# FNet mixing and an ELU feed-forward layer: the second batch's sequence transform in quarter form, and weight sums of two chunks at a time

## The chip, the cores and the metric

The kernel runs on one core of a Trainium2 chip. A core has a matrix engine (TensorE, PE), a vector engine (VectorE, DVE), a scalar engine (ScalarE, ACT), a general engine (GpSimd, POOL) and a queue for transfers (SyncE, SP). Each engine works through its own list of instructions, and semaphores order the lists against each other. The metric is device time in microseconds (us), the median of several executions; lower is better.

## The reference

`x` has 8 batches of 3008 rows (the sequence) by 256 channels in float32; `w_in` (256 x 2048) and `w_out` (2048 x 256) arrive in float64.

```python
X = np.fft.fft(x, axis=1)            # along the sequence, 3008 points
X = np.fft.fft(X, axis=2)            # along the channels, 256 points
y = X.real.astype(np.float32).reshape(8 * 3008, 256)
h = y @ w_in
g = np.where(h > 0.0, h, np.exp(np.minimum(h, 0.0)) - 1.0)
out = (g @ w_out).astype(np.float32)
```

## The kernel before

**The sequence transform.** The channel transform is multiplied into `w_in` once, when the weights are prepared (`fold_chunk`, into `Wc` and `Ws`). What is left is a real transform along the sequence for each batch, in two parts (cosines with channels folded evenly, sines with channels folded oddly) and each of these for even and odd frequencies: four transforms a batch, which the code names by `ri` (0 cosine, 1 sine) and `kodd` (0 even, 1 odd frequencies). GpSimd and VectorE first add and subtract rows of `x` that share a cosine, so that fewer rows are left to be multiplied. TensorE then multiplies the folded rows, which are its stationary operand, with a table of cosines, and VectorE unfolds the products into two ring buffers, `Rr` and `Ir`, of which each column is one frequency. A transform is done in two halves; a half is a group of matmuls into one bank `H`.

**Half form.** Batches 0 and 1 use it. The rows are split into six classes by their place modulo 8 and 4, folded twice, and lie in tiles `eo` of 128 rows; a half is three matmuls with the table `MC`: of 188, 188 and 376 columns in a first half, of some 376 columns each in a second half. In batch 1 the folding is 30 GpSimd operations (`mirror_folds`), spread over slots 6 to 30.

**Quarter form.** Batches 2 to 7 use it. The rows are split into eight classes (by their place modulo 8), of 96 and 94 rows; `near` (`far` = 0) and `far` tiles hold four classes each, as `xq0` to `xq3`. `load_quarter` and `load_odd` load them, by SyncE or by GpSimd's indirect transfers. GpSimd adds mirrored rows (`mirror_sum`), VectorE adds or subtracts the halves (`half_sum`, L627), GpSimd folds the channels (`channel_fold`, L630), ScalarE copies one column that has no partner (`channel_edge`, L633), VectorE and GpSimd combine classes (`quarter_pairs`, `shift_pairs`, `turn_pairs`; L911 is the vector engine's turn), and a half is then four matmuls of at most 95 columns with the smaller table `QM`.

**Slots.** The feed-forward layer works on 47 tiles of 256 frequencies, in 376 slots: a slot is one tile with two of the 16 blocks of 128 hidden features. In a slot TensorE forms `H` from `Rr` with `Wc` (called P here) and from `Ir` with `Ws` (Q); VectorE or ScalarE takes the part E between the two (`even_part`, L1401 on VectorE); VectorE forms the mirrored frequency's row as 2E - H (`h_minus`, L1415); ScalarE computes the exponentials (`below_plus` is the first of them, `G<-H`; then `M<-G`, `G<-G`, `M<-M`); VectorE finishes the ELU (`g_plus`, `g_minus`, L1431). TensorE then multiplies `G` with `w_out` into `pA` to `pD` (X below) one to two slots later. Slots 0 to 15 alternate between tiles 0 and 1, since the weights are still arriving, and multiply with plain products. From slot 16 a slot uses seven products (Winograd's form): GpSimd makes four sums of blocks of `G` in each slot (`G<-G`), and needs sums of `w_out`'s blocks (`sum_weights`, into `WT`), which it forms once, at slots 13 to 17: four operations for each of eight pairs of blocks.

**The weights.** They are turned from float64 to float32 on the chip in chunks, beside slots 0 to 14. Of each chunk VectorE takes two steps (`pow<-raw` L408 and `w<-raw` L420), ScalarE three (`pow<-pow,ebias`, `raw<-raw`, `w<-w`), GpSimd one (`w<-raw,w`), VectorE one (`pow<-raw,pow`, L462), GpSimd one (`w<-w,pow`). The four chunks 4 to 7 of `w_in` are also folded with the channel transform (`raw<-w` on GpSimd, a fold on TensorE, `Wsc<-H` on ScalarE). `spread_last_row` then sends one row of the result through memory into the columns `wex` (SyncE, `wx<-Wsc` at L673 and `wex<-wx` at L676), which E (and from slot 16 a seed on ScalarE) needs.

**Order.** The program is a list of events with a time each, in units of `T` = 4.8 us a slot; they are sorted by time and issued in that order. The times place instructions against each other on an engine's list; they do not make anything wait. So each engine's list is fixed by the table of times, and what an engine does when follows from the lists and the semaphores. The first 33 us have a table of their own (`FRONT`), in which `L` and `L0` to `L3` are the transfers of batch 1's rows.

## Time and profile before

| | |
|---|---|
| median of 3 runs | 1906.94 us (1906.89 to 1907.48) |
| profiled execution, its own time | 1907.16 us |
| its span in the trace | 1905.4 us |
| TensorE, matmuls | 1898.3 us busy, 8972 matmuls |
| VectorE | 1232.0 us busy |
| ScalarE | 1391.4 us busy |
| GpSimd | 1353.1 us busy |

The span is the time between the first and the last instruction in the trace; 1.76 us of the profiled execution's own time lie outside it. Rows of the trace give the start of a run of like instructions and its length in us, the engine, the source line, what is written and read, and how many instructions the run has (`x4`); in square brackets stands how long the engine was idle before and what it waited for. Each matmul stands in the trace as two records, so that `x6` is three matmuls. Since matmuls overlap, the price of a group of matmuls is the distance from its start to the next group's start, not its length. Before slot 34 and in the last slots TensorE is idle for some 10 us altogether; between them it never stops for more than a fraction of a microsecond.

### The profile page before, as it was taken

Reading aid. Unit: us, or ns where it says so; the run is one execution under the profiler, and the core shown is the slowest. Engines: PE = TensorE matmul, PEld = TensorE weight load, DVE = VectorE, ACT = ScalarE, POOL = GpSimd, SP = SyncE. Lnnn points to the kernel's source line nnn. Section 1 sums busy time; section 2 is a strip of 40 time slices with the busy share of each in tenths; the row PEclk is TensorE's granted clock in tenths of the full one; section 3 lists DMA queues with packets and bytes.
Section 4 is the critical chain, followed back from the end, with each engine's and each line's share of the span. In section 5 each row is a group of like instructions: output and inputs, shape, how many; then the busy total and the mean of one; then the engine's idle time right before and its main releaser. Section 6 shows DMA issues by size and latency. Waiting matters only on the chain.

```text
span 1905.4 us, 28620 instructions
## 1 busy us (share of the span) xinstructions
PE 1898.3 (100%) x8972; PEld 1656.8 (87%) x8972; DVE 1232.0 (65%) x2174; ACT 1391.4 (73%) x2803; POOL 1353.1 (71%) x1846
## 2 busy tenths in 40 slices
PE   9999999999999999999999999999999999999999
PEld 6888888888888888888888888888888888888887
DVE  8755555667666676667766677666776667655445
ACT  5767667777777777777777777777777777777775
POOL 4888658786687766777667777687766777556664
PEclk9999999999999999999999999999999999999999
DMA  8145211211011110211102111022110210100101
GB/s 340 45 33 43 55 24 45 53 24 36 12 44 41 32 33 12 47 40 30 31 19 50 35 27 31 13 56 44 24 24 16 55 21 15 17 12 15 20 11 24
DMA packets 278901, 73.66 MB, mean 39 GB/s; under 512 B 254382, under 2 KB 268972, under 8 KB 278750
## 3 DMA queue, kind: packets, MB, share of 16 engines
q1 hardware_dynamic: 270110, 61.40, 15.9%
q0 software_dynamic: 6464, 10.18, 1.7%
q8 instruction: 71, 1.16, 0.3%
q14 instruction: 80, 0.66, 0.1%
q10 hardware_dynamic: 2176, 0.26, 0.1%
HBM read 46.92 MB, written 24.80 MB: 38 GB/s over the span
## 4 chain that ended last, share of the span: by engine, by line
PE 96%; DVE 2%; ACT 1%; issue 0%; DMA 0%; POOL 0%; ACTq 0%; POOLq 0%; DVEq 0%
PE H L621 37%; PE pB L621 17%; PE pD L621 17%; PE pC L621 17%; PE pA L621 9%; DMA xl<-in_x_dram,ix 0%; DVE e L721 0%; ACT G L633 0%; DVE o L721 0%; POOL w L630 0%; DVE G L1431 0%; DVE E L1401 0%; ACT M L633 0%; ACT E L633 0%; DVE pow L462 0%
## 5 line engine op out<-in xcount | busy, mean ns | idle before, releaser
L630 POOL TENSOR_TENSOR G<-G 128x256 f32<-128x256 f32 x1437 | 1047.4, 737 | 498.0 <-DVE G L1431 358.5
L1431 DVE SCALAR_TENSOR_TENSOR G<-G,H 128x512 f32<-128x512 f32 x376 | 258.2, 687 | 554.5 <-ACT G L633 554.5
L633 ACT ACTIVATE G<-H 128x512 f32<-128x512 f32 x376 | 224.5, 597 | 259.0 <-DVE G L1415 255.4
L621 PE MATMUL H<-Rr,Wsc 128*128 128x256 f32 x1504 | 388.7, 381 | 1.0 <-ACT Wsc L633 0.5
L621 PE MATMUL H<-Ir,Wsc 128*128 128x256 f32 x1504 | 386.7, 380 | 0.7 <-DVE E L1401 0.7
L633 ACT ACTIVATE H<-Rb,wex 128x256 f32<-128x256 f32 x720 | 341.2, 474 | 40.0 <-DVE G L1431 21.5
L621 PE MATMUL pC<-G,WT 128*128 128x256 f32 x1440 | 369.8, 379 | 0.0
L633 ACT ACTIVATE E<-H 128x512 f32<-128x512 f32 x360 | 214.5, 596 | 182.0 <-PE H L621 181.7
L621 PEld LDWEIGHTS H<-Ir,Wsc 128*128 128x128 f32 x1504 | 285.6, 190 | 40.6 <-DVE E L1401 1.5
L621 PEld LDWEIGHTS H<-Rr,Wsc 128*128 128x128 f32 x1504 | 281.7, 190 | 43.1 <-issue 2.3
L621 PEld LDWEIGHTS pC<-G,WT 128*128 128x128 f32 x1440 | 274.2, 190 | 36.6
L1415 DVE SCALAR_TENSOR_TENSOR G<-E,H 128x512 f32<-128x512 f32 x376 | 255.0, 678 | 8.4 <-PE H L621 4.3
L1431 DVE SCALAR_TENSOR_TENSOR G<-M,G 128x512 f32<-128x512 f32 x376 | 256.7, 683 | 0.7 <-ACT M L633 0.7
L633 ACT ACTIVATE G<-G 128x512 f32<-128x512 f32 x376 | 235.0, 625 | 0.0
L621 PE MATMUL pA<-G,w 128*128 128x256 f32 x784 | 229.6, 380 | 0.1
L621 PE MATMUL pB<-G,w 128*128 128x256 f32 x784 | 229.5, 379 | 0.0
L621 PE MATMUL pD<-G,w 128*128 128x256 f32 x784 | 229.4, 379 | 0.0
L633 ACT ACTIVATE M<-G 128x512 f32<-128x512 f32 x376 | 224.4, 597 | 2.8 <-DVE G L1415 2.8
L633 ACT ACTIVATE M<-M 128x512 f32<-128x512 f32 x376 | 222.7, 592 | 0.1
L621 PE MATMUL pB<-G,WT 128*128 128x256 f32 x720 | 214.7, 380 | 0.0
L621 PE MATMUL pD<-G,WT 128*128 128x256 f32 x720 | 214.4, 379 | 0.0
L621 PEld LDWEIGHTS pA<-G,w 128*128 128x128 f32 x784 | 149.2, 190 | 20.6 <-DVE G L1431 0.5
(175 smaller groups left out, 1794.3 us busy)
## 6 DMA issues: line engine op xcount, KB each, us to landing
out_dram<-ot SPq DMA_DIRECT2D x496, 32.0 KB
xq<-in_x_dram SPq DMA_DIRECT2D x48, 94.0 KB
out_dram<-ot SPq DMA_DIRECT2D x256, 2.0 KB
Rb<-r SPq DMA_DIRECT2D x10, 376.0 KB
raw<-in_moe_w_in_dram SPq DMA_DIRECT2D x7, 512.0 KB
MC<-dft_mats SPq DMA_DIRECT2D x3, 943.5 KB
xq<-in_x_dram SPq DMA_DIRECT2D x12, 192.0 KB
xq<-in_x_dram SPq DMA_DIRECT2D x36, 64.0 KB
```

The lines of the kernel that those rows point to most:

```text
L621: nc.tensor.matmul(out_, lhsT=lhsT, rhs=rhs, start=start, stop=stop, skip_group_check=True)
L630: pin(nc.gpsimd.tensor_tensor(out=o, in0=a, in1=b, op=op))
L633: pin(nc.scalar.activation(out=o, in_=i, func=func, **kw))
L1415: nc.vector.scalar_tensor_tensor(out=two(S.G[:, 0:512])[:, :, ::-1], in0=two(S.E), scalar=2.0, in1=two(S.H), op0=ALU.mult, op1=ALU.subtract,)
L1431: nc.vector.scalar_tensor_tensor(out=o, in0=e, scalar=-1.0, in1=h, op0=ALU.add, op1=ALU.max)
```

## The change

Batch 1's transform takes the quarter form of batches 2 to 7. `mirror_folds` and its 30 GpSimd operations go; the loads of batch 1's rows, its folds, pairs and halves get places of their own from two tables (`FIRST`, `QUARTERS`), whose numbers are slots. Of the eight half sums two run on GpSimd, six on VectorE. In all batches a half sum is now one operation on two classes (96 x 2 x 256) where it was two (96 x 256 each). `sum_weights` handles two pairs of blocks in one operation: 16 operations of 128 x 256 in place of 32 of 128 x 128, at slots 13.2, 15.1, 16.4 and 17.3. The quarter tables `QM` are loaded at slots 18 to 30 instead of 51 to 60, which batch 2 needs later anyway. The number of halves of batch 1 stays eight; their places go from slots 26, 28, 34, 36, 37, 39, 42, 44 to slots 23, 25, 34, 36, 38, 40, 44, 46.

```diff
-        b11, b12 = w2v[:, 2 * i, 0:128], w2v[:, 2 * i, 128:256]
-        b21, b22 = w2v[:, 2 * i + 1, 0:128], w2v[:, 2 * i + 1, 128:256]
-        W = [t[:, i] for t in WT]
+        w = w2v[:, 2 * i : 2 * i + 4].rearrange("p (n r) (h c) -> p n r h c", r=2, h=2)
+        (b11, b12), (b21, b22) = ([w[:, :, r, h] for h in range(2)] for r in range(2))
+        W = [t[:, i : i + 2] for t in WT]
...
-    def mirror_folds(L):
...
-    def half_sum(kodd, far, h):
+    def half_sum(kodd, far, h, tt=vtt):
...
-        for m in (2 * h, 2 * h + 1):
-            vtt(o[:, 3 - m], a[:, m], b[:, m], ALU.subtract if kodd else ALU.add)
+        m = slice(2 * h, 2 * h + 2)
+        tt(o[:, 2 - 2 * h : 4 - 2 * h][:, ::-1], a[:, m], b[:, m], ALU.subtract if kodd else ALU.add)
...
-    names["L"] = lambda: [open_x(1)] + [state["loads"][n]() for n in (4, 5)]
-    for n in range(4):
-        names[f"L{n}"] = lambda n=n: state["loads"][n]()
+    def load_next(j):
+        load_quarter(1, j, 0)
+        if j in (0, 3):
+            load_odd(1, j, 0)
+
+    names["L"] = lambda: [load_next(0), load_next(3)]
+    names["L0"] = lambda: [quarter_table(), load_next(2)]
+    names["L1"] = lambda: load_next(1)
+    names["L2"] = lambda: [quarter_row(1), load_odd(1, 1, 0)]
+    names["L3"] = lambda: load_odd(1, 2, 0)
...
-    for i in range(8):
-        at((12.9 + 0.5 * i) * T + 3.6, lambda i=i: sum_weights(i))
+    for n, t in enumerate((13.208, 16.4467, 17.2731, 15.0726)):
+        at(t * T, lambda i=2 * n: sum_weights(i))
...
+    FIRST = (((10.3723, 'q', 0), (10.73, 'q', 3), (13.0128, 'q', 1), (11.9409, 'q', 2),
...
+    QUARTERS = ((23, 1, 0, 0, 29), (34, 0, 0, 0, 38), (38, 0, 1, 43, 48), (44, 1, 1, 45, 53))
...
-    at(34 * T, lambda: nc.sync.dma_start(out=twist_tab[0:96], in_=QT_dr.ap()))
-    for n in range(4):
-        at(
-            (51 + 3 * n) * T,
-            lambda n=n: load_quarter_mats(n % 2, n // 2),
-        )
-    first = (6, 6, 7, 7, 7, 7, 7, 8, 8, 8, 9, 9, 9, 9, 12, 15)
...
-    for n in range(30):
-        slot = first[n] if n < len(first) else n + 1
...
-    for step, ri, kodd in ((26, 0, 0), (34, 1, 0), (37, 0, 1), (42, 1, 1)):
-        at_dft(step, 2, 1, ri, kodd, lambda k=2 * ri + kodd: state["EO"][k])
+    at(20 * T, lambda: nc.sync.dma_start(out=twist_tab[0:96], in_=QT_dr.ap()))
+    for ri, kodd, step in ((1, 0, 18), (1, 1, 22), (0, 0, 30.3), (0, 1, 30.4)):
+        at(step * T, lambda ri=ri, kodd=kodd: load_quarter_mats(ri, kodd))
...
+    FAR_LOADS, MIRROR, HALVES, FOLDS, PAIRS = FIRST
+    for dt, fn, *key in FAR_LOADS:
+        at(dt * T, lambda fn={"q": load_quarter, "o": load_odd}[fn], key=key: fn(1, *key, 1))
+    for n, t in enumerate(MIRROR):
+        far, n = divmod(n, 8)
+        at(t * T, lambda n=n, far=far: mirror_sum((0, 3)[n // 4], far, (0, 2, 1, 3)[n % 4]))
+    for t, *key in HALVES:
+        at(t * T, lambda key=key: half_sum(*key[0:3], gtt if key[3] else vtt))
+    for t, ri, *key in FOLDS:
+        at(t * T, lambda ri=ri, key=key: channel_fold(ri, *key))
+        if key[2] and not ri:
+            at(t * T + 0.3, lambda key=key: channel_edge(*key[0:2]))
+    for t, fn, *key in PAIRS:
+        fn = {"p": quarter_pairs, "s": shift_pairs, "t": turn_pairs}[fn]
+        at(t * T, lambda fn=fn, key=key: fn(1, *key))
...
+    for step, ri, kodd, finish, join in QUARTERS:
+        at_quarter(step, 1, ri, kodd, finish, join)
```

Three places of the engines' lists show how the change moves instructions. The first is ScalarE's list around slot 11, whose `below_plus` is `G<-H`; the three rows ahead of it belong to the weights' last chunk of `w_in` (`w1`). Before:

```order
L633 ACTIVATE pow2_785<-pow2_785,ebias_71 128x512
L633 ACTIVATE raw_451<-raw_451 128x512
L633 ACTIVATE w1_450<-w1_450 128x2x256
L633 ACTIVATE G_828<-H_793 128x512
L633 ACTIVATE M_839<-G_828 128x512
```

With the change:

```order
L633 ACTIVATE pow2_807<-pow2_807,ebias_71 128x512
L633 ACTIVATE raw_460<-raw_460 128x512
L633 ACTIVATE w1_459<-w1_459 128x2x256
L633 ACTIVATE e_794<-xq1_529 96x4
L633 ACTIVATE e_847<-xq2_444 96x4
L633 ACTIVATE G_858<-H_815 128x512
L633 ACTIVATE M_877<-G_858 128x512
```

The two edge copies of batch 1's near tiles (`channel_edge`) now stand ahead of slot 11's `below_plus`. Each writes one column of a tile that GpSimd's channel folds write too.

The second is GpSimd's list at the same slots, where `w1` is the same chunk of `w_in` and `w2` a chunk of `w_out`. Before:

```order
L630 TENSOR_TENSOR w2_68<-w2_68,pow2_740 128x512
L630 TENSOR_TENSOR w1_450<-raw_451,w1_450 128x2x256
L630 TENSOR_TENSOR w1_450<-w1_450,pow2_785 128x2x256
L630 TENSOR_TENSOR raw_451<-w1_450 128x256 x2
L630 TENSOR_TENSOR bs_825<-side_768 1x188 x2
```

With the change:

```order
L303 DMA xq3_797<-in_x_dram,ix_66 94x768
L630 TENSOR_TENSOR e_801<-xq2_444 96x256
L630 TENSOR_TENSOR w1_459<-raw_460,w1_459 128x2x256
L630 TENSOR_TENSOR e_794<-xq1_529 96x256
L630 TENSOR_TENSOR w1_459<-w1_459,pow2_807 128x2x256
L630 TENSOR_TENSOR raw_460<-w1_459 128x256 x2
L630 TENSOR_TENSOR e_847<-xq2_444 96x256 x2
L630 TENSOR_TENSOR bs_855<-side_778 1x188 x2
```

Four channel folds of batch 1 now stand among the chunk's steps and right behind them; `e_847`, which ScalarE's second edge copy also writes, stands behind all of the chunk's steps.

The third is SyncE's list at slot 13, with the two transfers of `spread_last_row` for the last chunk. Before:

```order
L673 DMA wx_96<-Wsc_69 1x256
L676 DMA wex_70<-wx_96 128x2x1
L1214 DMA x1_938<-in_x_dram 8x192x1 x4
```

With the change:

```order
L673 DMA wx_96<-Wsc_69 1x256
L319 DMA xq1_929<-in_x_dram 80x2x256
L319 DMA xq1_929<-in_x_dram 14x2x256
L319 DMA xq1_929<-in_x_dram 32x2x256
L676 DMA wex_70<-wx_96 128x2x1
L319 DMA xq1_929<-in_x_dram 15x2x256
```

Three loads of batch 1's far rows now stand between the two transfers.

65 lines of the change are left out of this document (1 added, 64 removed).

## The prediction

> **What bounds the kernel now.** I read the page's busy times first, then its chain of waits, then the trace by stretches of time for each engine.
>
> ```profile
> PE 1898.3 (100%) x8972; PEld 1656.8 (87%) x8972; DVE 1232.0 (65%) x2174; ACT 1391.4 (73%) x2803; POOL 1353.1 (71%) x1846
> ```
>
> ```profile
> PE 96%; DVE 2%; ACT 1%; issue 0%; DMA 0%; POOL 0%; ACTq 0%; POOLq 0%; DVEq 0%
> ```
>
> TensorE is busy for the whole span and carries 96% of the chain that ends last. So two things move the end: matmul time that goes or comes, and any wait that reaches TensorE, since nothing behind such a wait is idle enough to take it up. Relief of the other engines is worth nothing unless one of their results arrives late at TensorE. The sum is made against the profiled execution's own 1907.16 us (span 1905.4 and 1.76 around it); the median is 0.22 lower.
>
> **The matmuls.** The rows of TensorE's timeline, one half of batch 1 of each length and one half of a quarter batch:
>
> ```profile
> 235.49 1.43 PE L621 MATMUL H<-MC,eo 128*128 128x188 f32 x6
> 236.75 1.03 PE L621 MATMUL H<-Rr,Wsc 128*128 128x256 f32 x4
> ...
> 246.25 2.06 PE L621 MATMUL H<-MC,eo 128*128 128x376 f32 x6
> 248.15 1.03 PE L621 MATMUL H<-Rr,Wsc 128*128 128x256 f32 x4
> ...
> 442.14 0.58 PE L621 MATMUL H<-QM,e 94*128 94x95 f32 x4
> 442.56 0.61 PE L621 MATMUL H<-QM,o 94*128 94x95 f32 x4
> 443.01 1.06 PE L621 MATMUL H<-Rr,Wsc 128*128 128x256 f32 x4
> ```
>
> From start to the next group's start, a first half takes 236.75 - 235.49 = 1.26, a second half 248.15 - 246.25 = 1.90, a quarter half 443.01 - 442.14 = 0.87 us. Batch 1 has four first and four second halves: 4 x 1.26 + 4 x 1.90 = 12.64 before, 8 x 0.87 = 6.96 after. **Term 1: -5.7 us.** The quarter half costs 0.109 us a record where the half form's cost follows its columns; the batches 2 to 7 already run it, so I take it as it is.
>
> **What the front pays.** Batch 1's new folding has to be done while the weights are still converted, in slots 8 to 16, where VectorE, ScalarE and GpSimd are tightly chained. I walked that stretch with the rows of before and the changed lists. VectorE's timeline:
>
> ```profile
> 80.09 0.87 DVE L1401 SCALAR_TENSOR_TENSOR E<-Rb,wex,H 128x256 f32<-128x256 f32 x2 [1.30 <-PE H L621]
> ...
> 87.46 0.87 DVE L1401 SCALAR_TENSOR_TENSOR E<-Rb,wex,H 128x256 f32<-128x256 f32 x2 [2.89 <-PE H L621]
> ...
> 90.40 0.67 DVE L1415 SCALAR_TENSOR_TENSOR G<-E,H 128x512 f32<-128x512 f32 x1
> ...
> 98.93 0.43 DVE L408 TENSOR_SCALAR pow<-raw 128x512 int32<-128x512 int32 x1 [2.15 <-POOL w L630]
> ...
> 102.14 2.31 DVE L462 SCALAR_TENSOR_TENSOR pow<-raw,pow 128x512 int32<-128x512 int32 x1
> 104.37 0.68 DVE L1415 SCALAR_TENSOR_TENSOR G<-E,H 128x512 f32<-128x512 f32 x1
> ...
> 111.64 0.87 DVE L1401 SCALAR_TENSOR_TENSOR E<-Rb,wex,H 128x256 f32<-128x256 f32 x2 [1.47 <-DMA wex<-wx]
> ```
>
> ```profile
> L627 DVE TENSOR_TENSOR xq<-xq,xq 96x256 f32<-96x256 f32 (+1 forms) x96 | 75.5, 823 | 0.0
> ```
>
> Four half sums of batch 1 now stand on VectorE in slots 8 to 10. No 96 x 2 x 256 form is in the trace. It moves as many elements a row as the 128x512 rows (0.67 us), and replaces two rows of 0.82 (1.65); I take the middle, 1.16, and keep 0.67 and 1.65. The first two vanish in the waits of 1.30 and 2.89 us for TensorE; the last two stand behind those waits and move the row at 90.40 by 2.3 (1.3 to 3.3, and nothing if the waits grow as TensorE runs on).
>
> Step by step from there; ScalarE first, then GpSimd:
>
> ```profile
> 95.56 0.61 ACT L633 ACTIVATE w<-w 128x512 f32<-128x512 int32 x1
> 96.81 0.60 ACT L633 ACTIVATE G<-H 128x512 f32<-128x512 f32 x1 [0.64 <-DVE G L1415]
> ...
> 105.08 0.60 ACT L633 ACTIVATE G<-H 128x512 f32<-128x512 f32 x1 [3.87 <-DVE G L1415]
> ...
> 107.12 1.18 ACT L633 ACTIVATE Wsc<-H 64x512 f32<-64x512 f32 x2
> ```
>
> ```profile
> 96.25 1.29 POOL L630 TENSOR_TENSOR w<-raw,w 128x512 f32<-128x512 f32 x1 [1.31 <-DVE pow L462]
> 97.63 1.27 POOL L630 TENSOR_TENSOR w<-w,pow 128x512 f32<-128x512 f32 x1
> 98.98 1.85 POOL L630 TENSOR_TENSOR raw<-w 128x256 f32<-128x256 f32 x2
> ```
>
> ```profile
> L630 POOL TENSOR_TENSOR e<-xq 96x256 f32<-96x256 f32 x48 | 40.4, 843 | 0.0
> ```
>
> 1. The last `w_in` chunk's ScalarE steps end at 96.17 (95.56 + 0.61); with VectorE 2.3 late at 98.5. GpSimd then does the round (96.25 to 97.63, 1.38), a channel fold (0.84), the multiply (1.35), the two `raw<-w` (1.81) and the two folds `e_847` (1.69): 7.07, so to 105.6.
> 2. ScalarE's second edge copy writes a column of `e_847`'s tile and has to wait for it, and `below_plus` of slot 11 stands behind it on the list. That row goes from 96.81 to 105.7. Even with VectorE in time it would be about 103.3. ScalarE's three exponentials behind it wait as well.
> 3. VectorE's `g_plus` of slot 11 waits for the first of them, 1.6 us later (107.3); with `g_plus`, `g_minus` and the weights' step at 102.14 (about 0.63 each if undisturbed) the next `h_minus` starts at 109.2, where it was 104.37.
> 4. From that row on before's distances hold: `below_plus` of slot 12 0.7 later (105.08), the weights' copy `Wsc` 2.04 behind it (107.12): 111.95. SyncE's two transfers follow:
>
> ```profile
> 108.33 0.23 SPq L673 DMA_DIRECT2D wx<-Wsc  x1
> 109.44 0.36 SPq L676 DMA_DIRECT2D wex<-wx  x1
> ```
>
> `wx` 1.21 behind the copy (113.2), `wex` 1.1 behind that, with three loads between them 1.2 (114.4), and E of slot 14 a further 2.20 (111.64 - 109.44): 116.6, where it was 111.64.
>
> ```profile
> 112.56 1.13 PE L621 MATMUL H<-Ir,Wsc 128*128 128x256 f32 x4
> ```
>
> 5. TensorE's Q of slot 14 starts 0.92 behind E's start, which is as soon as E's two instructions are done (112.51): it has no time to spare there. It moves from 112.56 to 117.5. **Term 2: +5.0 us.** Bounds: +2.6 with no VectorE lag (step 2's 103.3), +7.5 if half sums take 1.65 and step 102.14 again 2.31.
>
> [...]
>
> **Behind slot 14.** GpSimd's groups: the Winograd sums, and one of the three groups of the 32 weight sums:
>
> ```profile
> L630 POOL TENSOR_TENSOR G<-G 128x256 f32<-128x256 f32 x1437 | 1047.4, 737 | 498.0 <-DVE G L1431 358.5
> ...
> L630 POOL TENSOR_TENSOR WT<-w 128x128 f32<-128x128 f32 x16 | 7.8, 485 | 0.0
> ```
>
> 32 x 0.48 = 15.4 becomes 16 of the first row's shape, 11.8. But the last of them and a half sum of some 1.3 us stand among the first Winograd sums of slot 16. **Term 3: +0.3** (0 to 1.4). Everything later (the rest of the folds, pairs, loads of `QM`) I cost at 0, up to 1: GpSimd waited 358.5 us for VectorE over the whole run, in 376 slots about 1 us in each, and that idle time is the cover. All batches' half sums in one operation relieve VectorE alone, and pay nothing.
>
> Sum: 1907.16 - 5.7 + 5.0 + 0.3 = 1906.8, or 1906.5 against the median. **Forecast: 1906.5 us, no change that can be told.** From about 0.2% (3.8 us) on a difference can be told from none.
>
> **Rivals.**
> - **B, the whole gain.** The half sums hide, TensorE itself runs late enough in slots 8 to 12 that its waits take the lag, or ScalarE's edge copies come free sooner. For it: VectorE waits 1.30 and 2.89 us on TensorE, GpSimd idles 1.31 at 96.25. Against it: the fixed lists, by which `e_847` follows all of the chunk's steps. 1906.94 - 5.7 = 1901.3.
> - **C, slower: GpSimd's backlog holds SyncE.** The first load between `wx` and `wex` overwrites near rows of `xq1`, so it waits for the channel folds that read them; the last of these is GpSimd's fold behind the next `w_out` chunk's round. In my walk it ends at 112.5, only 0.7 before `wx` at 113.2. If each of the 18 GpSimd operations between 92 and 112 took 0.3 us longer beside a busy VectorE (the weights' step at 102.14 took 2.31 us, the row behind it of the same shape 0.68, so such stretching exists), the fold comes 5.4 late and `wex` 4.7: 1906.5 + 4.7 = 1911.2. It decides from 0.7 us of GpSimd lag on. Against it: the GpSimd rows of the same stretch before are near their means.
> - **D, no matmul gain.** 64 records at the mean weight load of the page (1656.8 / 8972 = 0.185 us) give 11.8, a saving of 0.8 instead of 5.7, and 1911.4. Against it: the four records at 442.14 take 0.42.
> - **E: the change doesn't do what it says**, batch 1's halves staying as long as before in another place: 1912.2, the forecast without term 1. Against it: the tables name 32 matmuls of the small size.
>
> **How the numbers follow.** The forecast 0.62, B 0.20, C 0.12, D 0.04, E 0.02. The forecast's own range is 1906.5 with term 2 between +2.6 and +7.5 and term 3 up to 1.4, and 1 for later: 1904 to 1911. Faster: B's 0.20 and 0.05 of the forecast's lower end. Slower: C, D and E with all but 0.04 of their 0.18, and 0.01 of the forecast's upper end. The rest, 0.60, is the same. The range for 8 in 10 takes in B's 1901.3 and C's 1911.2 nearly: 1901.2 to 1911.0.
>
> **What would show it.** Term 1: halves of batch 1 as `H<-QM` of 0.87 us, eight of them. Term 2: a ScalarE row `e<-xq` of 96x4 elements that waits for GpSimd until about 105, `G<-H` behind it, and TensorE waiting some 5 us in all between 100 and 118 us, last for VectorE's E behind `wex`. Term 3: GpSimd's sums near 130 us with TensorE waiting under 1 us. It would be wrong if ScalarE's wait ends near 97 (B), if SyncE's load rather than the `Wsc` copy releases `wex` (C), or if TensorE waits past slot 18 (something I costed at nothing).

## The result

| | before | with the change |
|---|---|---|
| median | 1906.91 us (1906.82 to 1907.48) | 1923.24 us (1921.57 to 1923.98, 4 runs) |
| profiled execution, its own time | 1907.16 us | 1923.98 us |
| its span | 1905.4 us | 1922.2 us |

The ratio is 1.0082 (95% interval 1.0069 to 1.0094): slower by some 16 us, where no change was forecast, and outside the range on record.

### The profile page after: what moved, and what is told of

It reads as the page before. It is cut to its first block, busy times and chain, and to the rows that moved or that the text cites. A ratio compares the mean times of both kernels' runs of the same rounds, so it can differ in the third digit from the quotient of the medians.

```text
span 1922.2 us, 28713 instructions
## 1 busy us (share of the span) xinstructions
PE 1898.3 (99%) x8988; PEld 1654.1 (86%) x8988; DVE 1234.9 (64%) x2190; ACT 1393.2 (72%) x2809; POOL 1371.2 (71%) x1844
## 3 DMA queue, kind: packets, MB, share of 16 engines
q8 instruction: 71, 1.16, 0.3%
## 4 chain that ended last, share of the span: by engine, by line
PE 92%; DVE 2%; DMA 2%; POOL 2%; ACT 1%; issue 1%; SPq 0%; ACTq 0%; POOLq 0%; DVEq 0%
PE H L621 36%; PE pB L621 16%; PE pD L621 16%; PE pC L621 16%; PE pA L621 8%; DMA xq<-in_x_dram,ix 1%; DMA wex<-wx 1%; POOL WT L630 0%; ACT G L633 0%; DMA xl<-in_x_dram,ix 0%; DVE G L1376 0%; POOL w L630 0%; POOL xq L630 0%; DVE e L721 0%; POOL G L630 0%
## 5 line engine op out<-in xcount | busy, mean ns | idle before, releaser
L630 POOL TENSOR_TENSOR G<-G 128x256 f32<-128x256 f32 x1437 | 1061.0, 746 | 482.3 <-DVE G L1376 345.7
L621 PEld LDWEIGHTS pB<-G,w 128*128 128x128 f32 x784 | 151.1, 193 | 21.2
```

The costliest lines, as they stand in the source:

```text
L621: nc.tensor.matmul(out_, lhsT=lhsT, rhs=rhs, start=start, stop=stop, skip_group_check=True)
L630: pin(nc.gpsimd.tensor_tensor(out=o, in0=a, in1=b, op=op))
```

## The profile after

The same two lines of the page as in the prediction, of the changed kernel (busy us per engine; the chain that ended last, by engine):

```profile
PE 1898.3 (99%) x8988; PEld 1654.1 (86%) x8988; DVE 1234.9 (64%) x2190; ACT 1393.2 (72%) x2809; POOL 1371.2 (71%) x1844
...
PE 92%; DVE 2%; DMA 2%; POOL 2%; ACT 1%; issue 1%; SPq 0%; ACTq 0%; POOLq 0%; DVEq 0%
```

The page counts records, and a matmul has two of them; so the 8972 of the table of before are records too, and the change has 16 more. TensorE is busy for 1898.3 us as before, though it has less to multiply, and the chain now holds 2% of transfers, where it held none. To find the place I take from TensorE's timeline the start of each slot (its four `H<-Rr,Wsc` records) in both traces and subtract. The differences of one slot to the next are what the slot lost:

| stretch | lost (us) |
|---|---|
| start of slot 0 | -0.41 |
| slot 4 | +6.50 |
| slots 8, 10, 11 | +1.25, +2.12, +1.05 |
| slot 12 | +10.24 |
| slot 14 | -0.27 |
| slots 15 to 22 | +0.62 |
| slots 23 to 47 (batch 1's halves) | -5.19 |
| slots 48 to the end | +0.9 |

With the last row (0.62 at slots 54 and 55, the rest behind the last slot) that is the span's 16.8 us. Two slots hold nearly all of the loss, and slot 14, where the prediction had its wait, holds none.

**Slots 4 and 12.** TensorE's timeline of before around slot 4, its P row of slot 4 being at 47.76 and of slot 5 at 53.81:

```profile
50.35 1.03 PE L621 MATMUL H<-Ir,Wsc 128*128 128x256 f32 x4
51.22 1.89 PE L621 MATMUL pB<-G,w 128*128 128x256 f32 x8
52.94 1.03 PE L621 MATMUL H<-raw,CC 128*128 128x256 f32 x4
53.81 1.03 PE L621 MATMUL H<-Rr,Wsc 128*128 128x256 f32 x4
```

The same rows of the changed kernel, and those of slot 12:

```profile
53.69 2.07 PE L621 MATMUL H<-Ir,Wsc 128*128 128x256 f32 x4 [3.58 <-DVE E L1346]
55.55 3.62 PE L621 MATMUL pB<-G,w 128*128 128x256 f32 x8
58.97 1.10 PE L621 MATMUL H<-raw,CC 128*128 128x256 f32 x4
...
119.77 2.08 PE L621 MATMUL H<-Ir,Wsc 128*128 128x256 f32 x4 [8.87 <-DVE E L1346]
121.64 3.05 PE L621 MATMUL pB<-G,w 128*128 128x256 f32 x8
124.52 1.03 PE L621 MATMUL H<-raw,CC 128*128 128x256 f32 x4
```

TensorE waits for E, 3.58 and 8.87 us. Then it pays a second time: right behind each wait the same matmuls take about twice as long (2.07 and 2.08 instead of 1.03). From the Q row to the row of `raw,CC` it is 58.97 - 53.69 = 5.28 and 124.52 - 119.77 = 4.75, where before had 52.94 - 50.35 = 2.59: 2.7 and 2.2 us on top. The windows of the trace show the granted clock, the share of full speed that TensorE was allowed (the number before the share of transfers), below 1.00 in the stretches around the two waits; it is 1.00 from 60 to 100 us:

```profile
35.00:60.00 25.00, 21.42 (x87) 0.86 0.48 132
60.00:100.00 40.00, 37.11 (x169) 1.00 0.09 24
100.00:128.00 28.00, 18.09 (x73) 0.82 0.27 81
```

This is also why TensorE's busy time did not fall: the 5.2 us saved at the halves come back as slow matmuls.

VectorE's rows of E in the changed kernel say what E waited for:

```profile
52.76 0.87 DVE L1346 SCALAR_TENSOR_TENSOR E<-Rb,wex,H 128x256 f32<-128x256 f32 x2 [4.77 <-DMA wex<-wx]
...
118.85 0.87 DVE L1346 SCALAR_TENSOR_TENSOR E<-Rb,wex,H 128x256 f32<-128x256 f32 x2 [6.52 <-DMA wex<-wx]
```

Both times it is the column transfer of `spread_last_row`, of chunk 2 and of chunk 6. SyncE's list of before at chunk 2:

```profile
43.71 0.28 SPq L673 DMA_DIRECT2D wx<-Wsc  x1
45.94 0.39 SPq L676 DMA_DIRECT2D wex<-wx  x1
```

and with the change, at chunk 2 and at chunk 6:

```profile
43.30 0.24 SPq L673 DMA_DIRECT2D wx<-Wsc  x1
43.66 2.31 SPq L336 DMA_DIRECT2D xq<-in_x_dram  x3
46.01 0.65 SPq L345 DMA_DIRECT2D xq<-in_x_dram  x1
46.77 0.39 SPq L676 DMA_DIRECT2D wex<-wx  x1
...
100.20 13.16 SPq L336 DMA_DIRECT2D xq<-in_x_dram  x3
113.47 0.41 SPq L673 DMA_DIRECT2D wx<-Wsc  x1
113.94 0.62 SPq L336 DMA_DIRECT2D xq<-in_x_dram  x1
116.72 0.39 SPq L676 DMA_DIRECT2D wex<-wx  x1
```

At chunk 2 four loads of odd rows stand between `wx` and `wex`, and the `QM` table of batch 1's first half right behind `wex` (issued at 47.20; the table of times has it at slot 18). The loads push `wex` back only 1.2 us against `wx`, but E starts 6.0 us behind `wex` (52.76 - 46.77). In before it started 2.9 us behind it (48.83 - 45.94), and then it had waited for TensorE and not for `wex`:

```profile
48.83 0.87 DVE L1401 SCALAR_TENSOR_TENSOR E<-Rb,wex,H 128x256 f32<-128x256 f32 x2 [0.44 <-PE H L621]
```

With the change VectorE is idle for 4.77 of the 6.0 us until the small transfer is there; with the loads behind `wex` slot 4 loses -0.01 (e1 below). At chunk 6 three such loads stand ahead of `wx` and hold the list for 13.16 us. The third of them adds the odd rows to a tile whose even rows an indirect transfer of GpSimd brings, and waits until that has landed:

```profile
100.42 1.52 POOL L303 DMA_INDIRECT xq<-in_x_dram,ix  x1 [0.85 <-DVE xq L627]
```

It landed at 112.70, 12.3 us after its issue, and `wx` followed at 113.47, though its data (`Wsc`) had been there since 105.8.

**What was forecast, and is there.** ScalarE's rows of the chunk's last step, the edge copies and `below_plus`:

```profile
107.00 0.61 ACT L633 ACTIVATE w<-w 128x512 f32<-128x512 int32 x1
...
109.81 0.21 ACT L633 ACTIVATE e<-xq 96x4 f32<-96x4 f32 x1 [2.20 <-POOL e L630]
114.53 0.21 ACT L633 ACTIVATE e<-xq 96x4 f32<-96x4 f32 x1 [4.51 <-POOL e L630]
114.77 0.60 ACT L633 ACTIVATE G<-H 128x512 f32<-128x512 f32 x1
```

The copies wait for GpSimd, and `below_plus` behind them starts at 114.77, 7.16 us after the chunk's last step has ended (107.61); the walk had 105.7 - 98.5 = 7.2. But that step ended 11.4 us later than in before (96.17). Slot 4's loss less the earlier start explains 6.1 of it; the other 5.3 stand against the 2.3 (1.3 to 3.3) that the walk gave VectorE. And a half of batch 1 in the new form, on TensorE:

```profile
180.72 0.36 PE L621 MATMUL H<-QM,e 95*128 95x95 f32 x2
180.92 0.61 PE L621 MATMUL H<-QM,o 94*128 94x95 f32 x4
181.37 0.39 PE L621 MATMUL H<-QM,e 94*128 94x94 f32 x2
181.59 1.06 PE L621 MATMUL H<-Rr,Wsc 128*128 128x256 f32 x4
```

181.59 - 180.72 = 0.87 us, the forecast price.

## The experiments

All runs in one table, worked out like the one above: median and range of the runs, ratio to before on the same chip with its 95% interval, and what TensorE lost per stretch in the profiled execution. The stretch 31 to 47 lost -4.13 in every kernel with the change's halves but e3 (4.67) and e5 (-3.92). A slot's loss can hold half clock behind a wait, 1.7 us in e8 and 2.7 and 2.2 in the change, and it came in one execution and not in another behind waits of like length (last section); differences of that size in one slot say nothing of an edit.

| kernel | median (range), us | ratio | slot 4 | 8-11 | 12 | 13-14 | 15-22 | 23-28 | 29-30 |
|---|---|---|---|---|---|---|---|---|---|
| the change | 1923.24 (1921.57-1923.98) | 1.0082 [1.0069, 1.0094] | 6.50 | 4.41 | 10.24 | -0.27 | 0.62 | -1.06 | 0.00 |
| e1 | 1918.69 (1918.41-1920.12) | 1.0061 [1.0044, 1.0077] | -0.01 | 4.41 | 10.33 | -0.27 | 0.66 | -1.05 | 0.00 |
| e2 | 1924.88 (1923.81-1926.17) | 1.0092 [1.0075, 1.0108] | 5.33 | 4.42 | 2.77 | 9.02 | 0.02 | -1.06 | 0.00 |
| e3 | 1916.43 (1913.71-1923.98) | 1.0042 [1.0025, 1.0059] | -0.01 | 4.42 | 4.88 | 1.88 | 0.79 | -1.05 | 0.45 |
| e4 | 1918.15 (1915.82-1925.30) | 1.0068 [1.0047, 1.0090] | 0.00 | 4.42 | 4.40 | 4.14 | 0.19 | -1.06 | 0.00 |
| e5 | 1921.15 (1917.04-1925.90) | 1.0065 [1.0047, 1.0082] | -0.01 | 4.40 | 3.27 | 1.87 | 0.83 | -1.06 | 11.54 |
| e6 | 1924.31 (1922.92-1924.75) | 1.0086 [1.0069, 1.0103] | 0.00 | 4.40 | 1.59 | 1.77 | 1.47 | 10.30 | 1.17 |
| e7 | 1922.94 (1917.75-1925.52) | 1.0081 [1.0060, 1.0102] | -0.01 | 4.39 | 2.13 | 1.80 | 1.49 | 5.49 | 1.17 |
| e8 | 1917.95 (1916.04-1923.52) | 1.0065 [1.0048, 1.0082] | -0.01 | 1.97 | 3.27 | 0.02 | 1.48 | 2.77 | 2.22 |
| e9 | 1911.61 (1910.31-1914.96) | 1.0025 [1.0015, 1.0035] | 0.00 | 1.43 | 3.25 | 0.95 | 2.93 | -1.06 | 0.00 |
| e10 | 1908.15 (1907.05-1909.20) | 1.0004 [0.9994, 1.0014] | 0.00 | 0.00 | 0.00 | 0.00 | -0.01 | 0.01 | 0.00 |
| e11 | 1918.69 (1916.58-1922.52) | 1.0057 [1.0043, 1.0071] | -0.01 | 0.81 | 0.70 | 13.46 | 0.00 | -1.06 | 5.00 |
| e12 | 1914.28 (1913.27-1918.60) | 1.0045 [1.0032, 1.0059] | 0.00 | 0.73 | 9.14 | -0.15 | 0.32 | -1.06 | 0.65 |
| e13 | 1917.84 (1917.12-1921.28) | 1.0055 [1.0042, 1.0068] | -0.01 | 0.94 | 0.67 | 1.71 | 10.59 | -1.06 | 4.26 |
| e14 | 1918.47 (1917.93-1922.62) | 1.0064 [1.0052, 1.0076] | -0.01 | 0.88 | 0.68 | 7.04 | 5.70 | -1.05 | 0.00 |
| e15 | 1915.56 (1914.07-1920.36) | 1.0050 [1.0036, 1.0064] | -0.01 | 0.85 | 0.70 | 1.54 | 6.53 | -1.06 | 1.39 |
| e16 | 1910.75 (1908.99-1912.21) | 1.0018 [1.0009, 1.0027] | -0.01 | 3.78 | 3.24 | 0.98 | 0.96 | -1.05 | -0.01 |
| e17 | 1919.13 (1916.04-1919.31) | 1.0058 [1.0044, 1.0072] | -0.01 | 0.98 | 3.14 | 0.20 | 2.04 | -1.06 | 10.40 |
| e18 | 1916.55 (1912.62-1918.33) | 1.0041 [1.0027, 1.0055] | -0.01 | 0.77 | 0.70 | 2.11 | 3.76 | -1.05 | 7.62 |

### SyncE's list: e1, e2, e3

e1 sends the loads of batch 1's near odd rows (and the `QM` tables and the table of the turn) only behind the latest `wex`:

```diff
+    def behind(fn, *key):
+        with tc.issue_after(state["wex"].ins):
+            return fn(*key)
...
-    names["L2"] = lambda: [quarter_row(1), load_odd(1, 1, 0)]
-    names["L3"] = lambda: load_odd(1, 2, 0)
+    names["L2"] = lambda: [quarter_row(1), behind(load_odd, 1, 1, 0)]
+    names["L3"] = lambda: behind(load_odd, 1, 2, 0)
```

> The changed kernel, but batch 1's odd near rows, the QM tables and the turn table are issued behind the pair wx, wex of chunk 3 (and later pairs) instead of between wx and wex of chunk 2. Theory S (transfers of batch 1 between a weight row's two transfers make E wait): the 6.5 us that slot 4 lost are gone, TensorE waits for E once less, 1923.2 - 6.5 = about 1916.7. Theory A (my forecast: the loss comes from ScalarE's edge copies alone): nothing changes, about 1923.

e2 does it for the far odd rows alone, which stood ahead of `wx` of chunk 6; e3 does both, and has the other far rows of `xq1` and `xq2` behind `wex` of chunk 7 too.

```diff
-    (10.8321, 'o', 0), (11.1884, 'o', 3)
+    (11.3, 'o', 0), (11.35, 'o', 3)
...
-        at(dt * T, lambda fn={"q": load_quarter, "o": load_odd}[fn], key=key: fn(1, *key, 1))
+        at(dt * T, lambda fn={"q": load_quarter, "o": load_odd}[fn], key=key:
+           (behind if fn is load_odd else lambda fn, *k: fn(*k))(fn, 1, *key, 1))
```

> The changed kernel, but the four odd far loads of xq0 and xq3, of which two wait for a GpSimd transfer, are issued behind wx and wex of chunk 6 instead of ahead of and between them. Theory S: E of slot 12 no longer waits for wex; what is left there is the wait for ScalarE's edge copies, which hold the next h_minus to about 118 us, so about 7 of the 10.2 us of slot 12 go: about 1916. Theory A: the edge copies hold the same stretch just as long, 1922 to 1923.

> Both edits together (and the far rows of xq1 behind wx and wex of chunk 7). Theory S: the gains add, 1923.2 - 6.5 - 7 = about 1910; what is left over the forecast's -5.7 is the edge copies' wait, +5 as in the forecast, and 2 to 4 of slots 8 to 11. Theory A: 1922 or more.

e1 takes slot 4's 6.50 us away, all of it, and leaves the other slots as they were: four loads between `wx` and `wex` and the table behind it cost 6.5 us together, of which 2.7 are TensorE's slow matmuls behind the wait. (The median fell by 4.6 only; 1916.7 was forecast.) e2 takes slot 12 from 10.24 to 2.77, so 7.5 us of that slot were SyncE's list, but the chip's time does not fall (1916 was forecast), since the next chunk now runs into the same thing. SyncE's rows, and VectorE's E of slot 14, in e2:

```profile
125.87 0.25 SPq L673 DMA_DIRECT2D wx<-Wsc  x1
...
127.76 1.27 SPq L676 DMA_DIRECT2D wex<-wx  x1
```

```profile
131.96 0.87 DVE L1350 SCALAR_TENSOR_TENSOR E<-Rb,wex,H 128x256 f32<-128x256 f32 x2 [7.59 <-DMA wex<-wx]
```

So SyncE's list is the cause at both slots, and the amount is set by what stands around the two small transfers. e3 missed its forecast of 1910 too: slots 12 to 14 still lose 6.8. In its profiled execution, which is its slowest (1923.98 of 1913.71 to 1923.98), 8.8 us more were lost at slots 34 and 35, where TensorE waited 6.62 us for `QM`, queued behind 41 stores; the profiled executions of e1 and e2, with the same lists from there on, did not have it.

### The edge copies of ScalarE: e4, e6, e7

e4 is e3 with the two edge copies a quarter to two thirds of a slot later, so that `below_plus` of slot 11 no longer waits behind them (one copy still waits, 1.15 us). e6 keeps them late and takes the transfers out of the way too (96 rows as in e5 below, and the loads of far rows behind `wex` of chunk 7; one far mirror sum moves with them); e7 is e6 with the edge copies back where the change has them.

```diff
-            at(t * T + 0.3, lambda key=key: channel_edge(*key[0:2]))
+            at(t * T + 0.3 if key[1] else 12 * T + 0.2, lambda key=key: channel_edge(*key[0:2]))
```

and for e6 and e7, of the far loads:

```diff
-    (13.0128, 'q', 1), (11.9409, 'q', 2), (12.5, 'o', 2)
+    (13.03, 'q', 1), (13.02, 'q', 2), (13.04, 'o', 2)
```

> As the run before, and ScalarE's two near edge copies behind slot 11's exponentials and the next chunk's three steps. If the edge copies cost what the forecast's walk gave (some 4 to 5 us on TensorE once the transfers are out of the way): about 1905, below the kernel before. If they cost nothing: the same as the run before.

> As the run with 96 rows, and the far rows of xq2, which stood ahead of wx and wex of chunk 7, behind them. If SyncE's list is what holds slot 14 (six loads of 0.4 us and a wait for Rb's row ahead of wx): slot 14's 4 us go, 1907 to 1909. If GpSimd then waits for these rows: the loss comes back at slot 16.

> As the run before, but with the edge copies where the change put them, ahead of slot 11's exponentials. Theory A's price, with the transfers out of the way: 4 to 5 us more than the run before. If the edge copies are hidden: the same.

e4 gains nothing against e3. Between e6 and e7 only the edge copies differ; slots 12 to 14 lose 1.59 + 1.77 = 3.36 and 2.13 + 1.80 = 3.93: 0.6 us for the wait that the prediction priced at 5.0. These are one profiled execution each, and 0.6 is within what executions differ by, but 5.0 is not. The forecast of e6 (slot 14's loss gone, 1907 to 1909) was missed: slots 13 and 14 went from e5's 1.87 to 1.77 only. Both have losses of their own at slots 24 to 30 (VectorE waited 12.3 us for a table that my edit had put behind the stores), so their medians say nothing of it.

### The rows of the indirect transfers: e5 and e14

e5 is e4 with far transfers of 96 rows instead of 94 (two rows that nothing uses come along); it also issues the two `QM` tables of `ri` 0 from ScalarE. e14 and e13 (below) differ in these rows alone.

```diff
-            n = 94 if far else 96
+            n = 96
...
-                    element_offset=(b * SEQ + (HALF if j in (1, 3) else 0) + i) * ND,
+                    element_offset=(b * SEQ + (HALF if j in (1, 3) else 0) + i - 16 * far) * ND,
```

> As the run with the edge copies later (medians 1918, slot 12 still 4.4 us and slot 14 still 4.1 us late), but GpSimd's far transfers fetch 96 rows instead of 94 (two rows more, unused), and the two QM tables of slot 34 are issued from ScalarE's queue. Theory D (a transfer of 94 rows lands slowly, 12.3 and 8.7 us here against 3.7 to 4.9 of 96 rows, and wx and wex, which share its DMA engines, wait for it: 3.4 to 4.0 us from wx to wex instead of 1.1): the far transfers land in about 4 us, wx to wex takes 1.1 to 2 us, TensorE's wait in slot 12 goes nearly, 1911 to 1913. Theory Q (only the order in SyncE's queue matters): the transfers and the waits of slots 12 and 14 stay as they were; only the rare 7 us wait at slot 34 goes.

> As e13, but with the far transfers of 94 rows of the change, not of 96. Theory S with the rows as a cause of their own: they land in 9 to 12 us instead of 3.5, the loads that wait for them now stand behind wex of chunk 7, so they hold up the loads of x for slot 19 and on, not a chunk: 0 to 2 us over e13. Rival U (the rows cost by themselves, through engines that a slow transfer occupies, wherever it is issued): wx of chunks 6 and 7 takes 4 us or more to its wex, as in the change, instead of 1.9, and the time is 4 us or more over e13.

The view of transfers between 90 and 112 us, for e4 (packets, MB and share of 16 engines of GpSimd's queue; then median us from issue to landing):

```profile
q0 software_dynamic: 800, 0.58, 8.5%
...
xq<-in_x_dram,ix POOLq DMA_INDIRECT x2, 9.0
```

and for e5:

```profile
q0 software_dynamic: 128, 0.59, 8.2%
...
xq<-in_x_dram,ix POOLq DMA_INDIRECT x2, 3.5
```

As many bytes go in 128 packets instead of 800 and land in 3.5 us instead of 9.0. The trace of before has both sizes in batches 2 to 7: there the transfers of 94 rows landed 8.7 to 9.7 us after their issue, those of 96 rows 3.3 to 5.2. Why 94 rows are slower, no run shows.

What 94 rows do to others is shown by e13 and e14, where the same lists run. SyncE's rows of chunk 7 in e13:

```profile
111.15 0.24 SPq L673 DMA_DIRECT2D wx<-Wsc  x1
112.42 0.36 SPq L676 DMA_DIRECT2D wex<-wx  x1
```

and in e14, with two 94-row transfers under way since 108.8:

```profile
111.97 0.24 SPq L673 DMA_DIRECT2D wx<-Wsc  x1
116.71 0.36 SPq L676 DMA_DIRECT2D wex<-wx  x1
```

`wex` reads what the 1 KB `wx` has written to memory, so it goes out when `wx` has landed: 4.74 us after `wx` instead of 1.27. E of slot 14 waits 4.43 us for `wex`, where it waits 1.65 in e13, and the slot loses 7.04 instead of 1.71. So rival U has its 4 us from `wx` to `wex` at that slot, behind slow transfers that do not stand ahead of the small ones on SyncE's list; that engines in common are the reason was a guess, and no run shows it. The medians are only 0.6 us apart, by which theory S would stand; but e13 loses more at slots 18 and 29 (below), and the slots decide. In e5 the slots behave so as well: slot 12 falls from e4's 4.40 to 3.27, slots 13 and 14 from 4.14 to 1.87. Its median is 1921.15 and not the 1911 to 1913 of its forecast, since ScalarE's list, with the `QM` that I had put there, was held for 12.2 us at slot 30, a cost of that edit alone.

### The sums that come late: e8 and e9

Once the transfers are out of the way, slots 8 to 11 still lose 4.4 us. e8 is e6 with five near mirror sums 0.3 to 0.7 slots earlier on GpSimd. e9 also puts folds of near rows behind the chunk's steps, three far half sums and two far mirror sums 0.5 to 1.4 slots later, and the tables early (`QM` of slot 34 from GpSimd).

```diff
-    8.9733, 8.5167, 8.7263, 7.2198, 7.5248, 7.27, 7.5, 7.6557
+    8.9733, 8.5167, 8.7263, 6.9, 6.92, 6.91, 6.93, 6.94
```

and for e9 also (mirror sums, half sums, and the first of the folds):

```diff
-    16.73, 17.4075
-    (17.4576, 0, 1, 0, 0), (17.8288, 0, 1, 1, 1), (17.7099, 1, 1, 0, 0)
-    (10.6784, 0, 0, 0, 0), (11.3098, 0, 0, 0, 1)
+    18.08, 18.09
+    (18.25, 0, 1, 0, 0), (18.3, 0, 1, 1, 1), (18.3, 1, 1, 0, 0)
+    (11.62, 0, 0, 0, 0), (11.625, 0, 0, 0, 1)
```

> As the run with the far rows behind wex of chunk 7, and the first five of GpSimd's near mirror sums ahead of the chunk's step for which GpSimd waits 6.1 us at slot 7, instead of behind it. If these sums cause the 1.25 us of slot 8 (TensorE waits 0.98 us for raw) and a part of the 3.2 us of slots 10 and 11: 2 to 4 us less than that run. If GpSimd waits for the rows instead: nothing gained or slower.

> The run with the early mirror sums, and in it: the turn table and the QM tables of slots 23 and 44 behind wex of chunks 3 and 4 (early), the QM table of slot 34 from GpSimd's queue, the five near channel folds behind GpSimd's steps of the w_in chunk instead of among them, and the last far mirror sums, far half sums and folds behind the Winograd sums of slots 16 and 17. If what is left in the run with the early mirror sums (slot 11 1.05, slot 12 3.3, slot 18 1.6, slot 24 3.6, slot 30 2.2 us) are waits of these places, nearly all of its 12 us above the matmuls' gain go: 1903 to 1907, at or below the kernel before. If transfers or GpSimd are simply too full in slots 8 to 18, the waits move elsewhere and it stays at 1912 or more.

e8 takes slots 8 to 11 from 4.40 to 1.97: there VectorE's half sums had waited for GpSimd's mirror sums, as this row of the changed kernel shows:

```profile
90.28 1.24 DVE L627 TENSOR_TENSOR xq<-xq,xq 96x512 f32<-96x512 f32 x1 [1.93 <-POOL xq L630]
```

Slot 12 rises from 1.59 to 3.27 at the same time, behind the same wait of TensorE (2.29 and 2.28 us): in e8 the clock is halved behind it, in e6 not (last section). e9 is the first kernel near the time of before, 1911.61 us, but still slower by 0.25% (0.15 to 0.35). Its forecast had 1903 to 1907, or 1912 and more. Part of what it loses at slot 12 is VectorE behind GpSimd's weight steps; VectorE's row in e9:

```profile
101.47 0.43 DVE L408 TENSOR_SCALAR pow<-raw 128x512 int32<-128x512 int32 x1 [2.52 <-POOL w L630]
```

Before waits there too (2.15 us at 98.93). Beyond the 0.97 by which TensorE is late already, the row stands 1.57 us later than in before, and the half clock behind TensorE's wait of 2.26 us adds 1.7 (4.38 us from the Q row to that of `raw,CC`, 2.69 in e6); together that is slot 12's 3.25 to 0.02.

### The two small parts: e10

The kernel before with the `sum_weights` and `half_sum` parts of the diff alone: weight sums of two pairs at a time, at the change's places, and half sums in one operation.

```diff
-    for i in range(8):
-        at((12.9 + 0.5 * i) * T + 3.6, lambda i=i: sum_weights(i))
+    for n, t in enumerate((13.208, 16.4467, 17.2731, 15.0726)):
+        at(t * T, lambda i=2 * n: sum_weights(i))
...
-        for m in (2 * h, 2 * h + 1):
-            vtt(o[:, 3 - m], a[:, m], b[:, m], ALU.subtract if kodd else ALU.add)
+        m = slice(2 * h, 2 * h + 2)
+        vtt(o[:, 2 - 2 * h : 4 - 2 * h][:, ::-1], a[:, m], b[:, m], ALU.subtract if kodd else ALU.add)
```

> The kernel before, with the two small parts of the change alone: weight sums of two pairs of blocks in 16 operations, and half sums as one operation of 96 x 512 in batches 2 to 7. The forecast cost both at nothing (within 0.3): about 1907. If the weight sums of slot 16 held GpSimd's Winograd sums (the 0.7 us of slot 18 in the changed kernel), 1907.5 to 1908; if relief of VectorE helped, below 1906.5.

1908.15 against 1907.21 us, no difference that can be told. No slot up to 47 loses more than 0.01 us, and the later ones lose 0.56 in all. The two parts have no part in the loss, as costed.

### Can the rest be placed away? e11, e12, e16

e11 moves e9's near half sums of the odd classes to slot 11.75, its far ones to 19.2, and the far transfers and the loads behind them 1 to 1.5 slots later; e12 moves the sums alone; e16 moves only the far sums and what reads them.

```diff
-    (10.3723, 'q', 0), (10.73, 'q', 3), (11.3, 'o', 0), (11.35, 'o', 3)
-    (10.2482, 1, 0, 0, 0), (10.27, 1, 0, 1, 0), (18.25, 0, 1, 0, 0), (18.3, 1, 1, 0, 0)
+    (11.83, 'q', 0), (11.85, 'q', 3), (12.4, 'o', 0), (12.45, 'o', 3)
+    (11.75, 1, 0, 0, 0), (11.76, 1, 0, 1, 0), (19.2, 0, 1, 0, 0), (19.25, 1, 1, 0, 0)
```

> The kernel of e9 with more places moved: the two near half sums of the odd classes to slot 11.75, the far half sums of VectorE to slot 19.2, the folds of the near classes either side of them, the pair sums that follow later, and the indirect far transfers with the loads that wait for them some 1.5 slots later. Theory P (what is left over in e9 at slots 12 to 21 are waits for the mirror sums of GpSimd and for the half sums of VectorE, each at its place): the 3.2 us at slot 12 and the 1.9 at slot 19 go to under 1 us each, nothing new comes, and the time falls from 1911.6 to 1905 to 1908, about the kernel before or under it. Rival R (the work of batch 1 that is now on VectorE and GpSimd costs this much wherever it stands, since VectorE's chain of a chunk has no room in these slots): the waits move by one or two slots with their sum, 4 to 7 us, unchanged; 1910 to 1914. A load that waits for a far transfer now stands ahead of wx of chunk 7: if that holds the chunk up, slot 14 gains 3 to 8 us, and the time says nothing of P or R.

> As the run before, but with the transfers and their loads where e9 has them, so that only the sums, folds and pair sums of VectorE and GpSimd are moved. Theory P: 1905 to 1908, with slots 12 and 19 under 1 us each. Rival R: 1910 to 1914, the same 4 to 7 us of waits one or two slots on. Against the run before it tells what the later transfers cost or save by themselves: the same time within 1 us if they hold nothing, 3 to 8 us less if wx of chunk 7 is held there.

> As e9, and of e12's moves only those behind slot 18: the far half sums of VectorE to slot 19.2 and the folds and pair sums that read them up to 1 slot later; the near half sums stay where e9 has them. Theory S: the 3.25 us at slot 12 stay, the 1.90 at slot 19 and the 1.04 at slot 21 go (e12 showed 0.01 and 0.32 there), so 2 to 3 us less than e9: 1908 to 1910, or 1907 to 1908 with slot 14's 0.95 gone too. Rival T: the two waits go elsewhere, 1911 to 1913.

None of the three forecasts held in time: e11 came to 1918.69, by the exception that its text names for slot 14, e12 to 1914.28, and e16 to 1910.75, just above its 1908 to 1910. e11 shows slot 12 at 0.70 and slots 15 to 22 at 0.00, so these losses were indeed places; but the loads that wait for the far transfers again stood ahead of `wx` of chunk 7, and slot 14 lost 13.46. In e12 the half sums came too late for GpSimd's first far transfer, which overwrites what they read; GpSimd's row, and VectorE's half sums that it waits for:

```profile
98.94 0.94 POOL L303 DMA_INDIRECT xq<-in_x_dram,ix  x1 [8.52 <-DVE xq L627]
```

```profile
97.39 1.28 DVE L627 TENSOR_TENSOR xq<-xq,xq 96x512 f32<-96x512 f32 x2
```

GpSimd stood still for 8.52 us with the chunk's weight steps queued behind the transfer; VectorE's next step waited 7.89 us for them, and slot 12 lost 9.14. e16 has slots 15 to 22 at 0.96 instead of 2.93, as said, but its slots 8 to 11 lost 3.78 instead of e9's 1.43, though the lists are the same up to slot 18: GpSimd waited 0.69 us for the weights' step on VectorE (L462) at 73.81 in e16, where it has no wait in e9, and TensorE then waited for E 1.86 us in e16 (77.08) and 0.58 in e9 (75.85). So one execution of such a kernel differs from the next by 2 us there. 1910.75 us is the lowest median of all runs with the new form, 0.18% (0.09 to 0.27) above before.

### GpSimd's room and SyncE's: e13, e15, e17, e18

e13 is e11 with the loads of far odd rows behind `wex` of chunk 7 and the mirror sums that need them later. e15 puts these loads behind three loads of `x`, and six mirror sums behind the first sums of `G`'s blocks (`G<-G`) of slot 18. e17 is e15 with these six sums on VectorE, one half sum moved, and the loads ahead of those of `x`. e18 is e17 with the loads where e15 has them.

The places against e11 in e13, e15 and e17 (loads of far odd rows, then mirror sums), and e17's operation:

```diff
-    (12.4, 'o', 0), (12.45, 'o', 3) | 18.08, 18.09, 14.951, 15.9599, 14.3361, 14.0108, 14.8731, 14.2
+    (13.035, 'o', 0), (13.036, 'o', 3) | 18.08, 18.09, 15.3, 15.9599, 14.3361, 14.0108, 15.0, 15.2
+    (15.7, 'o', 0), (15.75, 'o', 3) | 18.08, 18.09, 18.1, 18.11, 14.3361, 14.0108, 18.12, 18.13
+    (13.06, 'o', 0), (13.065, 'o', 3) | 16.6, 17.2, 18.2, 18.25, 14.3361, 14.0108, 18.6, 18.65
...
-    def mirror_sum(j, far, m):
+    def mirror_sum(j, far, m, tt=gtt):
...
-        gtt(own[:, m, 1:], own[:, m, 1:], other[:, m, :0:-1], ALU.add)
+        tt(own[:, m, 1:], own[:, m, 1:], other[:, m, :0:-1], ALU.add)
```

> As e11, but the three loads of odd rows that wait for a far transfer stand behind wex of chunk 7, and the mirror sums that read them come up to 1.7 slots later. Theory S (the whole of what e11 loses at slot 14 is SyncE's list, and batch 1's new work has room on the four other engines): slot 14 goes from 13.5 to under 1 us, the lag at slot 22 is 1.5 to 3 us instead of 15, the new form's own gain of some 5 us stands in full behind it, and the time is 1902.5 to 1906, under the kernel before for the first time. Rival T (the work has no room, and each place that is mended opens the next one): 3 us or more appear at a new slot between 14 and 30, and the time is 1907.5 to 1912.

> As e13, but the four loads of odd far rows stand behind the loads of the even ones and three of the loads of x, and all six mirror sums that no earlier step needs stand behind the first four twists of G at slot 18, so that GpSimd waits for no transfer ahead of them. Theory S (the loss is all in places): slots 8 to 22 lose 0.8 + 0.7 + 1.7 and no more, a lag of 3 to 5 us at slot 22, and the new form's 5 us behind it make 1902.5 to 1907. Rival T (each place that is mended opens the next): 3 us or more at a new slot, 1908 to 1916.

> As e15, but six of the eight far mirror sums of batch 1 run on VectorE instead of GpSimd, two in slots 16 and 17 and four in slot 18, and the four loads of odd far rows stand ahead of the loads of x and behind all others. Theory V (what moves from place to place in e9, e12, e13 and e15 is one thing: GpSimd has no room from slot 13 to 20, where it works without a gap in e15 from 107.5 to 139.1 us, so every mirror sum put there delays a weight sum or a twist by its own length): with six sums of 0.6 to 0.8 us gone from GpSimd, slot 19 goes from 6.54 to under 1.5 us, the lag at slot 22 from 9.1 to 3 to 4.5, and the time to 1904 to 1908, so that the forecast gain of the matrix multiplications comes through. Rival T (any engine that takes the sums passes on the wait: VectorE's chain of a chunk is as full): 4 us or more at slots 16 to 19, 1910 to 1916.

> As e17, with the four loads of odd far rows back behind three loads of x, as in e15, and the sums that read them half a slot to a slot later, on VectorE still. In e17 slot 19 lost 0.41 us instead of 6.54, but slots 29 and 30 lost 10.4: the loads of x took SyncE 13.32 us there instead of 5.98 (e9), its list stayed some 12 us late, and the extra rows of slot 30 came late. Theory W (that is the whole of it, and the loss of the change is SyncE's list and GpSimd's room at named places, behind which the forecast gain stands): slots 29 and 30 lose 1 to 2 us as in e15, slots 18 to 22 no more than 3, and the time is 1905 to 1909.5, at or under the kernel before. Rival T (no placing of these loads leaves both the chunk and the extra rows alone): 5 us or more at one slot, 1911 to 1918.

In time none was as fast as its theory said: e15 and e18 came out in their rivals' ranges, e13 and e17 above them. Slot by slot they say more. e13's slot 14 falls from 13.46 to 1.71, so e11's loss there was the list. But at slot 18 GpSimd waited for a transfer with the sums of `G`'s blocks behind it (the trace names a load of `x` as the last to come):

```profile
130.43 0.89 POOL L630 TENSOR_TENSOR xq<-xq,xq 94x255 f32<-94x255 f32 x2 [7.07 <-DMA x<-in_x_dram]
```

In e15 no slot up to 18 loses more than 1.6 us, and slot 19 loses 6.54: TensorE waits for a sum of `G`'s blocks, which stands behind six mirror sums (and their wait of 1.5 us for a transfer).

```profile
144.95 0.48 PE L621 MATMUL pB<-G,WT 128*128 128x256 f32 x1 [4.58 <-POOL G L630]
```

With these sums on VectorE slot 19 loses 0.41 (e17) and, with the loads where e15 has them, 0.63 (e18): GpSimd's room was the cause at that slot, theory V as far as it goes. The time was lost again ten slots on. SyncE's loads of `x`, which before slot 30 give the extra rows, took 5.98 us in e9:

```profile
120.77 5.98 SPq L1163 DMA_DIRECT2D x<-in_x_dram  x4
```

and in e17, straight behind the four loads of odd rows:

```profile
125.36 13.32 SPq L1163 DMA_DIRECT2D x<-in_x_dram  x4
```

GpSimd then waited in e17 for the extra rows of slot 30 (the bracket names `xq`, but what the operation reads is `xs`, whose transfer SyncE could issue only at 200.13):

```profile
203.15 0.39 POOL L630 TENSOR_TENSOR xs<-xs 128x96 f32<-128x96 f32 x1 [10.27 <-DMA xq<-in_x_dram]
```

e18, with the order of e15 there, still lost 7.62 at slots 29 and 30, where e15 lost 1.39 from nearly the same list. So theory W fell. Each stretch is nearly free of loss in some kernel (slot 4 in e1, slots 8 to 11 at 0.73 in e12, slot 12 at 0.67 in e13, slots 13 and 14 at 0.02 in e8, slots 15 to 22 at 0.00 in e11, where a lag of 15 us went ahead, slots 29 and 30 in e9), but in no kernel all of them. Whether the lists have an order in which they all are stays open, and so does why e18 lost more than e15 at slot 29.

## Why the prediction was wrong

- **Term 1, the matmuls (-5.7): right in mechanism, nearly in size.** Slots 23 to 47 gave -5.19 in the change, and -1.06 and -4.13 in its two parts (to 0.01) in twelve of the kernels above too. The new halves cost 0.87 each. The old first half at slot 26 gave back 1.02, not 1.26, and small remainders of 0.1 make up the rest.
- **Term 2, +5.0 by ScalarE's edge copy (steps 1 to 5): the step that failed is step 5, by which the delay of `below_plus` comes out whole at TensorE's Q of slot 14.** Steps 1 and 2 are there on GpSimd (7.16 us against 7.2); VectorE's lag ahead of them was 5.3 and not 2.3. But slots 13 and 14 lost -0.27 in place of +5.0. TensorE was held at slot 12 already: the exponentials behind the edge copies had ended at 116.89, and E of slot 12 had to wait for `wex` of chunk 6 until 118.85, so their delay lay inside that wait. With `wex` in time the copies cost 0.6 us (e6 against e7). In e7 VectorE's list has two waits in a row there, 3.19 us for GpSimd's weights and then 3.34 for the exponentials; that the first takes up most of the second is argued from this, not tested.
- **What the walk left out.** It looked at SyncE's list at chunk 7 alone, found three loads that cost 1.2 us to issue, and costed loads by their issue; chunks 2 and 6 it put at nothing, without a reason. Loads of the same kind stood between `wx` and `wex` of chunk 2 and ahead of `wx` of chunk 6. There they cost 6.5 us (e1, together with the table behind them) and 7.5 of slot 12's 10.2 us (e2). Two things make up the price, and the prediction has a term for neither. The indirect transfers of 94 rows landed late, 12.3 us after the issue at chunk 6; the trace of before has 8.7 to 9.7 us for those of the later batches, and it was not read. And TensorE ran at half clock (0.50) behind the two waits, which cost 2.7 and 2.2 us; before has no case of it in these slots (granted clock 1.00 from 30 to 128 us).
- **The half sums of VectorE** cost what was taken (1.21 and 1.24 us alone, 2.38 for two, against 1.16), but "the first two vanish in the waits" was wrong: slots 8 to 11 lost 4.41 us at TensorE. e8 shows that 2.4 of it were mirror sums of GpSimd, for which the prediction has no step; what the other 2 us are, no run separates.
- **Term 3 and what was costed at 0.** The small parts cost nothing (e10). "Everything later at 0, up to 1" was right for the change (0.62 at slots 15 to 22), where TensorE was 20 us late by then and GpSimd had so much more time. In e9 and in e11 to e18, where the lag is smaller, these slots and 29 and 30 lose up to 10.6 us a stretch. The average idle time of 1 us a slot was no proof of room at a certain slot.
- **Rival C** was the nearest: SyncE held by a load that waits for GpSimd. It named chunk 7 and a fold; it was chunk 6 and a far transfer, at twice the price.
